# The last V of a decode attention: from four loads and single-column matmuls to one load and four-column matmuls, with the FFN between its parts

## The chip, the cores and the metric

The kernel runs on one core of a Trainium2 chip. The metric is device time of one execution in microseconds, as the median of the fast runs. "Span" is the time from the first to the last instruction of one profiled execution; it is about 2 us less than that execution's time (the profiled run of before: span 1285.6, time 1287.6). Ratios are the mean time of one kernel's fast runs over the mean of the other kernel's fast runs of the same rounds, with a 95% interval, so they are not quite the ratio of the medians quoted beside them.

## The reference

One token of decode: layer norm of x (640), attention with 32 heads over a cache of 32768 positions with head size 128, and beside it a SwiGLU FFN with 1728 hidden units on the same normalised x; everything is added.

```python
xn = layernorm(x)
q = (xn @ wq)                     # 32 heads x 128
p = softmax(q @ k.T * 128**-0.5)  # per head, 32768 keys
o = p @ v                         # per head
out = x + concat(o) @ wo + (silu(xn @ w_gate) * (xn @ w_up)) @ w_down
```

All tensors are bf16. K and V are 8 MiB per head each; everything together is 554 MB, read once.

## The kernel before

K and V of the heads pass through a ring of three 8 MiB slots. A head's scores are made by VectorE (multiply) and TensorE (sum over the head dimension by an identity matmul). Probabilities P lie with key `p * 256 + j` at partition p, column j. V is multiplied in two ways. For heads 0 to 30, four columns j are taken at once ("four-column form"): the weights are 128x4, the moving data are 512 columns of V, and the wanted sums are the four diagonal blocks of a 4x512 result. ScalarE evacuates it (`o4`) and `fold` adds the blocks. (This cut and the two after it are shortened; comments are added.)

```python
PARTS = [64, 64, 128]; W = 4
def pv_part(h, part):
    ...  # part 0 waits for P, for the bank O to be evacuated, and for V
    for j in range(first, first + PARTS[part], W):
        mm = t.matmul(O, lhsT=P[:, h % PR, j:j + W], rhs=ring[:, s, j * DH:(j + W) * DH],
                      start=(j == 0), stop=(j + W == NJ))

def fold(h):   # four fp32 matmuls
    for m in range(W):
        mm = t.matmul(fold_ps, lhsT=o4[:, m * DH:(m + 1) * DH], rhs=identf[0:W, m:m + 1], ...)
```

Head 31 is different: its V comes in four loads, and V itself is the weight, with one column of P as moving data ("single-column form"). That gives the output as a column, without evacuation and fold.

```python
TAIL = [128, 64, 32, 32]          # 4, 2, 1, 1 MiB, a semaphore each
def pv_last(pieces):
    for i in pieces:
        t.wait_ge(s_tail[i], 16)
        for _ in range(TAIL[i]):
            mm = t.matmul(OL, lhsT=ring[:, s, j * DH:(j + 1) * DH], rhs=P[:, h % PR, j:j + 1],
                          start=(j == 0), stop=(j == NJ - 1))
            j += 1
```

Behind V of head 31 the load queue takes gate, up and down weights and then Wo in six pieces. TensorE's tail:

```python
total(H - 1)
pv_last([0])
fold(H - 2)
pv_last(range(1, len(TAIL))).then_inc(s_pv, 1)
hidden_part(0)                        # gate: 70 single-column matmuls, weights strided by 13 elements
t.wait_ge(s_ob, 1)
t.matmul(op, lhsT=oblk, rhs=fold32)   # transposes all heads' outputs into rows for Wo
hidden_part(1).then_inc(s_f, 1)       # up
down()                                # after SiLU on ScalarE and VectorE
project().then_inc(s_att, 1)          # 160 matmuls, waits for six Wo pieces
```

## Time and profile before

| What | Value |
|---|---|
| time | 1287.2 us median (1287.11 to 1287.53, 4 runs) |
| loads | DMA row full in 39 of 40 slices, 431 GB/s over the span |
| TensorE in the tail (1252.8 to 1283.3) | waits 0.6, 1.9 and 0.7 us for Wo, 0.20 and 1.34 us for "issue" |

From the page of the kernel before, the busy share of the DMA engines in 40 equal slices (9 is 90% or more), the granted TensorE clock in tenths, and one of the instruction queues (packets, MB, share):

```profile
PEclk9799888999888898888998888998888998888995
DMA  9999999999999999999999999999999999999998
q8 instruction: 9, 0.15, 0.0%
```

The loads never pause, so a shorter kernel needs either fewer bytes or a shorter tail behind the last of them.

The chain of waits of the kernel before, near its end (start, us, what; the last two pieces, 0.6 us, are left out):

```profile
1253.03 28.77 DMA ring<-in_A_wo_dram
1281.80 0.05 issue
1281.85 1.49 PE ps L428 x40
```

The chain ends in a Wo load: Wo sets the time, and 1.5 us of matmuls plus 2.3 us of fixed work follow.

TensorE's instructions of the kernel before in order of time (start, us, engine, line, out<-in, shape, count, idle before and what ended it). L349 is V of head 31, L359 a fold, L403 gate and up, L412 down, L428 the projection:

```profile
1252.83 3.46 PE L349 MATMUL ps<-P,ring 128*128 128x1 bf16 x128
1256.22 1.86 PE L359 MATMUL ps<-identf,o 4*128 4x1 f32 x8
1258.01 1.20 PE L349 MATMUL ps<-P,ring 128*128 128x1 bf16 x39
1259.41 2.53 PE L349 MATMUL ps<-P,ring 128*128 128x1 bf16 x89 [0.20 <-issue]
1261.80 2.47 PE L403 MATMUL ps<-xn,ring 128*128 128x1 bf16 x39
1265.61 1.83 PE L403 MATMUL ps<-xn,ring 128*128 128x1 bf16 x31 [1.34 <-issue]
1267.33 4.13 PE L403 MATMUL ps<-xn,ring 128*128 128x1 bf16 x70
1272.92 1.87 PE L412 MATMUL ps<-hcol,ring 128*128 128x1 bf16 x65 [1.46 <-DVE hcol L615]
1276.80 1.23 PE L428 MATMUL ps<-ot,ring 128*128 128x1 bf16 x40 [0.59 <-DMA ring<-in_A_wo_dram]
1279.89 1.22 PE L428 MATMUL ps<-ot,ring 128*128 128x1 bf16 x40 [1.86 <-DMA ring<-in_A_wo_dram]
1281.85 1.48 PE L428 MATMUL ps<-ot,ring 128*128 128x1 bf16 x40 [0.74 <-DMA ring<-in_A_wo_dram]
```

256 matmuls on V take 7.2 us, about 28 ns each, and the two gaps without a cause ("issue") sit exactly 256 instructions apart (89 + 39 matmuls, a weight load and a matmul each).

### The profile page before, as it was taken

What the parts mean: (1) busy time and instruction counts of PE and PEld (TensorE: products, weight loads), DVE (VectorE), ACT (ScalarE), POOL (GpSimd) and SP (SyncE); (2) the same over time, 40 slices, a digit from 0 to 9 for tenths busy, and PEclk for the clock granted to TensorE, in tenths of its full rate; (3) what the DMA queues carried; (4) which work ended last, traced back from release to release, by engine and by line L of the source; (5) the groups of instructions that cost most, each with busy time, mean ns of one, the idle gap of its engine ahead of it and who ended that gap; (6) DMA issues with size and microseconds to landing.
All of it is one profiled execution on the core that took longest, in us unless ns stands there. A gap on an engine that the chain in (4) does not pass through costs nothing.

```text
span 1285.6 us, 9851 instructions
## 1 busy us (share of the span) xinstructions
PE 1042.0 (81%) x5154; PEld 260.9 (20%) x3235; DVE 672.2 (52%) x409; ACT 52.1 (4%) x139; POOL 2.5 (0%) x17
## 2 busy tenths in 40 slices
PE   3599777889787799778788777898777798778797
PEld 1012112221112221112221112221112221112227
DVE  0855665445665446664446664446664446654441
ACT  2000000000000000000000000000000000000000
POOL 0000000000000000000000000000000000000000
PEclk9799888999888898888998888998888998888995
DMA  9999999999999999999999999999999999999998
GB/s 424 425 445 433 427 430 441 428 432 440 432 432 428 440 430 430 442 430 432 428 440 430 430 442 430 432 428 440 430 430 442 430 432 428 440 430 430 442 413 365
DMA packets 11256, 554.17 MB, mean 431 GB/s; under 512 B 1259, under 2 KB 1516, under 8 KB 1772
## 3 DMA queue, kind: packets, MB, share of 16 engines
q1 hardware_dynamic: 11242, 554.00, 99.7%
q8 instruction: 9, 0.15, 0.0%
q14 instruction: 3, 0.02, 0.0%
q10 hardware_dynamic: 2, 0.00, 0.0%
HBM read 553.99 MB, written 0.00 MB: 431 GB/s over the span
## 4 chain that ended last, share of the span: by engine, by line
DMA 53%; PE 28%; DVE 12%; issue 6%; SPq 0%; DVEq 0%
DMA ring<-in_A_k_cache_dram 51%; PE ps L337 17%; DVE ring L554 12%; PE ps L305 9%; DMA ring<-in_A_wo_dram 2%; PE ps L324 1%; PE ps L379 0%; PE ps L373 0%; PE ps L367 0%; PE ps L428 0%; SPq L249 0%; DVEq L554 0%; DVE sc L560 0%; DVE pmax L566 0%; DVE m L569 0%
## 5 line engine op out<-in xcount | busy, mean ns | idle before, releaser
L554 DVE TENSOR_TENSOR ring<-ring,qb 128x8192 bf16<-128x8192 bf16 x128 | 557.8, 4420 | 315.6 <-DMA ring<-in_A_k_cache_dram 315.6
L305 PE MATMUL ps<-ring,ident 128*128 128x512 bf16 x1920 | 498.4, 418 | 0.0
L337 PE MATMUL ps<-ring,P 128*4 128x512 bf16 x1984 | 443.3, 379 | 0.0
L324 PE MATMUL ps<-ring,ident 128*128 128x512 bf16 x128 | 56.1, 439 | 220.1 <-DVE ring L554 219.7
L337 PEld LDWEIGHTS ps<-ring,P 128*4 128x4 bf16 x1984 | 163.4, 85 | 237.8
L324 PEld LDWEIGHTS ps<-ring,ident 128*128 128x128 bf16 x128 | 12.6, 99 | 618.3 <-DVE ring L554 359.5
L560 DVE TENSOR_REDUCE sc<-ps 128x64 f32<-128x512 f32 x128 | 82.2, 683 | 63.4 <-PE ps L305 63.4
L572 DVE TENSOR_SCALAR negb<-ps 128x1 f32<-128x1 f32 x32 | 5.1, 159 | 108.4 <-PE ps L379 108.4
L480 ACT ACTIVATE P<-sc,negb 128x256 bf16<-128x256 f32 x32 | 16.2, 507 | 957.7 <-DVE negb L572 957.7
L569 DVE TENSOR_REDUCE m<-ps 1x1 f32<-1x128 f32 x32 | 8.9, 279 | 85.2 <-PE ps L373 85.2
L359 PEld LDWEIGHTS ps<-identf,o 4*128 4x128 f32 x248 | 30.7, 190 | 13.1 <-issue 13.1
L359 PE MATMUL ps<-identf,o 4*128 4x1 f32 x248 | 33.3, 251 | 0.0
L367 PEld LDWEIGHTS ps<-rsum,ones 128*128 128x128 f32 x64 | 12.1, 190 | 99.7 <-issue 98.9
L471 ACT ACTIVATE o<-ps,rzb 4x512 f32<-4x512 f32 x31 | 21.0, 678 | 6.2 <-PE ps L337 6.2
L297 PE MATMUL ps<-ring 128*128 128x512 bf16 x39 | 10.4, 428 | 10.8 <-DMA ring<-in_A_wq_dram 10.7
L476 ACT ACTIVATE ocol<-ps 128x1 f32 (+1 forms) x31 | 5.4, 173 | 222.4 <-PE ps L359 222.4
L566 DVE TENSOR_REDUCE pmax<-sc 128x1 f32<-128x256 f32 x32 | 13.4, 420 | 0.0
L373 PE MATMUL ps<-identf,pmax 128*1 128x128 f32 x64 | 12.2, 273 | 1.2 <-DVE pmax L566 1.2
L379 PE MATMUL ps<-m,ones 1*128 1x1 f32 x64 | 12.1, 256 | 0.4 <-DVE m L569 0.4
L379 PEld LDWEIGHTS ps<-m,ones 1*128 1x128 f32 x64 | 9.4, 182 | 14.2 <-issue 13.5
L403 PE MATMUL ps<-xn,ring 128*128 128x1 bf16 x140 | 8.3, 196 | 1.3 <-issue 1.3
L542 DVE RECIPROCAL rzb<-ps 128x1 f32<-128x1 f32 x32 | 5.0, 157 | 8.1 <-PE ps L367 8.1
(66 smaller groups left out, 82.5 us busy)
## 6 DMA issues: line engine op xcount, KB each, us to landing
ring<-in_A_wq_dram SPq DMA_DIRECT2D x1, 5120.0 KB, 15.2
ring<-in_A_v_cache_dram SPq DMA_DIRECT2D x1, 4096.0 KB, 31.8
ring<-in_A_wo_dram SPq DMA_DIRECT2D x3, 1280.0 KB, 24.7
ring<-in_B_w_gate_dram SPq DMA_DIRECT2D x1, 2160.0 KB, 23.2
ring<-in_B_w_up_dram SPq DMA_DIRECT2D x1, 2160.0 KB, 27.9
ring<-in_B_w_down_dram SPq DMA_DIRECT2D x1, 2080.0 KB, 31.3
ring<-in_A_v_cache_dram SPq DMA_DIRECT2D x1, 2048.0 KB, 36.4
ring<-in_A_v_cache_dram SPq DMA_DIRECT2D x2, 1024.0 KB, 39.4
```

The source lines that it names most:

```text
L305: return t.add_instruction(mybir.InstMatmult(start_tensor_calc=False, stop_tensor_calc=stop, tile_size=(128, 128), tile_position=(0, 0), l ...
L324: t.matmul(ob, lhsT=ident[:, :], rhs=src, start=True, stop=False)
L337: mm = t.matmul(O, lhsT=P[:, h % PR, j:j + W], rhs=ring[:, s, j * DH:(j + W) * DH], start=(j == 0), stop=(j + W == NJ))
L359: mm = t.matmul(fold_ps, lhsT=o4[:, m * DH:(m + 1) * DH], rhs=identf[0:W, m:m + 1], start=(m == 0), stop=(m == W - 1))
L367: t.matmul(misc[:, 129:130], lhsT=ones[:, :], rhs=rsum[:, h % SR:h % SR + 1], start=True, stop=True).then_inc(s_z, 1)
L373: t.matmul(misc[0:1, 0:128], lhsT=pmax[:, h % SR:h % SR + 1], rhs=identf[:, :], start=True, stop=True).then_inc(s_t, 1)
L379: t.matmul(misc[:, 128:129], lhsT=ones[0:1, :], rhs=m1[0:1, h % SR:h % SR + 1], start=True, stop=True).then_inc(s_b, 1)
L471: a.activation(out=o4[:, :], in_=O, func=ACTF.Copy, scale=rzb[0:W, h % SR:h % SR + 1]).then_inc(s_o4, 1)
L480: a.activation(out=P[:, h % PR, :], in_=sc[:, :], func=ACTF.Exp, bias=negb[:, h % SR:h % SR + 1], scale=c_scale, accum_out=rsum[:, h % SR: ...
L554: v.tensor_tensor(out=kh, in0=kh, in1=q[:, None, :].to_broadcast([128, HF, DH]), op=ALU.mult).then_inc(s_mul, 1)
L560: v.tensor_reduce(out=sc[:, i * HF:(i + 1) * HF], in_=bank[i].rearrange("p (j e) -> p j e", e=G), axis=AX.X, op=ALU.add).then_inc(s_red, 1)
L566: v.tensor_reduce(out=pmax[:, h % SR:h % SR + 1], in_=sc[:, :], axis=AX.X, op=ALU.max).then_inc(s_max, 1)
```

## The change

The intent: treat the last head like the others, so that the tail has one load instead of four and 192 fewer matmuls with as many weight loads, and use gate and up to fill the time between V's parts.

```diff
-                    elif u == LASTV:
-                        ...                      # four loads
                     elif u[0] == "v":            # now head 31 too: one 8 MiB load
 ...
                 total(H - 1)
-                pv_last([0])
+                pv_part(H - 1, 0)
                 fold(H - 2)
-                pv_last(range(1, len(TAIL))).then_inc(s_pv, 1)
+                pv_part(H - 1, 1)
                 hidden_part(0)
+                pv_part(H - 1, 2)
+                hidden_part(1).then_inc(s_f, 1)
+                fold(H - 1)
+                down()
                 t.wait_ge(s_const, 5 + 2 * RB)
                 t.wait_ge(s_ob, 1)
                 t.matmul(op, lhsT=oblk[:, :, :], rhs=fold32[:, :], start=True, stop=True).then_inc(s_op, 1)
-                hidden_part(1).then_inc(s_f, 1)
-                down()
                 t.wait_ge(s_ot, 1)
                 project().then_inc(s_att, 1)
```

(Cut: ScalarE evacuates and copies the column of head 31 as for the others; VectorE builds `oblk` after `hcol`; `acc` moves to bank 1, because `fold_ps` is still in use.)

More of the change, by code (lines that the diff above doesn't have):

```diff
@@ L46, in bass_parallel_sum__gqa_block_cached__swiglu_ffn__decode_kernel @@
     SR = 3
-    TAIL = [128, 64, 32, 32]
     RB = DH // 32
@@ L52, in bass_parallel_sum__gqa_block_cached__swiglu_ffn__decode_kernel @@
     W = 512 // DH
-    assert sum(TAIL) == NJ and sum(PARTS) == NJ and NHF == 4 and (H - H0) % PER == 0 and PER % SLOTS == 0
+    assert sum(PARTS) == NJ and NHF == 4 and (H - H0) % PER == 0 and PER % SLOTS == 0
     assert PER % PR == 0 and PER % SR == 0
@@ L76, in bass_parallel_sum__gqa_block_cached__swiglu_ffn__decode_kernel @@
     WQ_S, FFN_S, WO_S = slot_of[("wq",)], slot_of[("ffn",)], slot_of[("wo",)]
-    LASTV = ("v", H - 1)
     with ExitStack() as es:
@@ L120, in bass_parallel_sum__gqa_block_cached__swiglu_ffn__decode_kernel @@
         s_ffn = [sem(n) for n in ("gate", "up", "down")]
-        s_tail = [sem(f"tail{i}") for i in range(len(TAIL))]
         s_const = sem("const")
@@ L208, in bass_parallel_sum__gqa_block_cached__swiglu_ffn__decode_kernel @@
             O = ps8[0:W, 4, :]
-            OL = ps8[:, 5, 0:1]
             op = ps8[:, 5, 8:8 + OC]
-            acc = ps8[:, 6, 0:NCD]
+            acc = bank[1][:, 0:NCD]
             fold_ps = ps8[:, 6, 8:9]
@@ L228, in sp @@
                         owner[s] = (s_qk, NHF * (u[1] + 1))
-                    elif u == LASTV:
-                        j = 0
-                        for i, n in enumerate(TAIL):
-                            e.dma_start(ring[:, s, j * DH:(j + n) * DH],
-                                        kv_src(A_v_cache, u[1], j, n)).then_inc(s_tail[i], 16)
-                            j += n
                     elif u[0] == "v":
@@ L340, in pv_part @@
                         mm.then_inc(s_pv, 1)
-                def pv_last(pieces):
-                    h = H - 1
-                    s = slot_of[LASTV]
-                    for i in pieces:
-                        t.wait_ge(s_tail[i], 16)
-                        j = sum(TAIL[:i])
-                        for _ in range(TAIL[i]):
-                            mm = t.matmul(OL, lhsT=ring[:, s, j * DH:(j + 1) * DH], rhs=P[:, h % PR, j:j + 1],
-                                          start=(j == 0), stop=(j == NJ - 1))
-                            j += 1
-                    return mm
                 def fold(h):
@@ L500, in act @@
                 column(H - 2)
+                evac(H - 1)
+                a.wait_ge(s_f, 1)
+                a.activation(out=sg[:, 0, :], in_=ffn[:, 0:FB], func=ACTF.Exp, scale=-1.0).then_inc(s_fa, 1)
+                column(H - 1)
                 a.wait_ge(s_op, 1)
                 a.activation(out=ot[:, :], in_=op, func=ACTF.Copy).then_inc(s_ot, 1)
-                a.wait_ge(s_f, 1)
-                a.activation(out=sg[:, 0, :], in_=ffn[:, 0:FB], func=ACTF.Exp, scale=-1.0).then_inc(s_fa, 1)
             @block.vector
@@ L592, in dve @@
                 twice(0)
-                h = H - 1
-                v.wait_ge(s_pv, H)
-                v.wait_ge(s_rz, H)
-                v.tensor_scalar(out=ocol[:, h:h + 1], in0=OL, scalar1=rzb[:, h % SR:h % SR + 1],
-                                scalar2=None, op0=ALU.mult).then_inc(s_ov, 1)
+                twice(1)
                 v.wait_ge(s_const, 5 + 2 * RB)
-                v.wait_ge(s_ov, H + 1)
-                v.tensor_tensor(out=oblk[:, :, :], in0=ocol[:, :, None].to_broadcast([128, H, RB]),
-                                in1=blk[:, None, :].to_broadcast([128, H, RB]), op=ALU.mult).then_inc(s_ob, 1)
-                twice(1)
                 v.tensor_reduce(out=par[:, :], in_=ident[:, :].rearrange("p (f t) -> p t f", t=2),
@@ L616, in dve @@
                                 scalar2=ffn[:, FB + FM:2 * FB], op0=ALU.mult, op1=ALU.mult).then_inc(s_fd, 1)
+                v.wait_ge(s_ov, H + 1)
+                v.tensor_tensor(out=oblk[:, :, :], in0=ocol[:, :, None].to_broadcast([128, H, RB]),
+                                in1=blk[:, None, :].to_broadcast([128, H, RB]), op=ALU.mult).then_inc(s_ob, 1)
                 v.wait_ge(s_xr, 1)
```

## The prediction

> **What bounds the kernel now.** The load stream. The DMA row of the 40 slices is full to the end, at 431 GB/s over the span; the chain of waits ends in a 28.8 us wait for the last Wo load, and the instructions in order of time show the projection waiting 0.6, 1.9 and 0.7 us for Wo pieces until 1281.8 us; 2.3 us more of fixed work follow its last matmul. The tail's loads (11.9 MB of FFN weights and Wo) come behind V of head 31, which lands at about 1254.5 us (issues at 1213.0 to 1214.3 plus 31.8 to 40.4 us), exactly one K and one V period (38.7 us) after the last K. So splitting that load costs no visible bandwidth, and joining it gains none; Wo still lands at about 1281.8.
>
> **What the change does to TensorE.** It has little slack in the tail.
> - Removed: 256 single-column matmuls at 27 to 28 ns (7.2 us). Half of them ran before V had wholly landed (1252.8 to 1256.3). Added: 64 four-column matmuls at 221 ns warm (16 took 3.54 us, 32 took 7.01): 14.1 us, all after 1254.5. That is 6.9 us more work and about 1.8 us later start.
> - Code fetch: the tail shows two gaps put down to issue, 0.20 and 1.34 us, exactly 256 instructions apart. [...]
> - Clock: [...]granted clock drops at 1216.8, rises at 1223.6, drops at 1254.3, all multiples of 3.41 us apart, and it then stays 0.5 through single-column work. Now that matters: part 0 of the last V may begin cold, and gate (4.1 us of single-column work) may cool it before part 2. [...]
> - The op matmul and its copy move behind down, onto the path: about 0.55 us.
>
> **Sum along TensorE.** V at 1254.5; part 0 3.5; fold 1.1; part 1 3.5; gate 4.1; part 2 7.0; up 4.1; SiLU chain to down 1.5 (read: 1271.46 to 1272.92), the last fold hidden in it; down 2.1; op and copy 0.55; projection 4.7; end 2.3. That gives 1289.0 us warm, 1292 with both cold starts, against a span of 1285.6 before. Wo, landed at 1281.8, is then waited for no more: the limit moves from the loads to TensorE. With the 1.7 us between span and measured time: 1290.7 to 1293.7. Strided gate and up weights took 59 ns each at half clock and may be faster warm, up to 2 us.
>
> **Predicted:** 1292.0 us, range 1289.5 to 1294.5; slower by 0.4%. Chances: faster by over 2% 0.01, within 2% 0.97, slower 0.02.
>
> **Shows it right:** everything up to 1250 us unchanged; V landing near 1254.5 and part 0 starting there; 64 matmuls of 128x512 taking 14 to 17.5 us; no wait of the projection on Wo, whose landing stays near 1282; chain of waits ending in PE lines rather than Wo; issue gaps of gate and up gone.
>
> **Would make it wrong:** V's single load landing much later or earlier than 1254.5; gate and up running at 30 ns when warm (1289 to 1290); the clock staying cold through all of part 2 (then 1295 or more); a fetch stall within the projection, whose 320 instructions run at 29 ns; Wo still ending the chain, so that the time hardly moves (1287 to 1288).

The sum came to 1289.0 us without cold starts and 1292 with both; the term for a cold start, up to 1.7 us each, was the author's estimate. The trace of the kernel before bears out the size roughly, but not as a bound: 128x512 matmuls that began at a granted clock of 0.50 at 1220.4, 1181.7 and 1143.1 us stayed there for 3.2, 4.3 and 5.4 us (windows view), some 430 ns apart instead of 221, so they lost about half of that, 1.6 to 2.7 us (an estimate from these numbers). That the 1.5 us of issue gaps would go was a forecast; the sum has gate at 4.1 us, without a gap.

## The result, and the profile after

1294.16 us median (1293.42 to 1294.9, 4 runs) against 1287.2 (1287.11 to 1287.53, 4 runs): ratio 1.0054, 95% interval 1.0036 to 1.0071.

The chain of waits of the changed kernel, from the last load in it (start, us, what; L327 is the four-column form, L337 a fold, L381 gate and up, L390 and L396 down, L406 the projection; a VectorE step before down and the pieces after the projection are left out):

```profile
1212.89 41.49 DMA ring<-in_A_v_cache_dram
1254.38 0.14 issue
1254.51 5.10 PE ps L327 x16
1259.62 0.98 PE ps L337 x8
1260.60 3.54 PE ps L327 x16
1264.14 4.11 PE ps L381 x70
1268.25 8.48 PE ps L327 x32
1276.73 4.12 PE ps L381 x70
1282.30 1.87 PE ps L390 x65
1284.17 0.35 PE ps L396 x6
1284.85 4.47 PE ps L406 x160
```

No Wo load is left in the chain. From the landing of V on, it is TensorE without a pause except the 1.4 us of SiLU (between 1280.85 and 1282.30, in which TensorE does the last fold) and 0.5 us for the op matmul and its copy.

TensorE in order of time, the two places that answer to the gaps and to the Wo waits before:

```profile
1264.07 4.18 PE L381 MATMUL ps<-xn,ring 128*128 128x1 bf16 x70
1284.85 4.46 PE L406 MATMUL ps<-ot,ring 128*128 128x1 bf16 x160 [0.29 <-ACT ot L486]
```

Gate is in one piece (the 1.34 us gap is gone) and the projection runs through in one piece: all of Wo had landed.

The windows view of the changed kernel (stretch, its us, busy us of the engines, granted clock in the third last column):

```profile
1254.00:1255.00 1.00, 0.49 (x2) 0.22 (x3) 0.00 (x0) 0.00 (x0) 0.00 (x0) 0.58 0.93 397
1257.00:1258.00 1.00, 1.00 (x5) 0.40 (x4) 0.00 (x0) 0.00 (x0) 0.00 (x0) 0.72 1.02 432
1267.00:1268.00 1.00, 1.00 (x20) 1.00 (x20) 0.00 (x0) 0.00 (x0) 0.00 (x0) 0.90 1.11 455
1268.00:1269.00 1.00, 1.00 (x10) 0.39 (x10) 0.00 (x0) 0.00 (x0) 0.00 (x0) 0.50 0.84 348
1271.00:1272.00 1.00, 1.00 (x5) 0.38 (x4) 0.00 (x0) 0.00 (x0) 0.00 (x0) 0.89 0.95 399
```

The clock halves at about 1254.2 and comes back at 1257.6, and again from 1267.8 to 1271.2 (worked out from the mean clock of the microseconds in which it changed): both times just before a stretch of four-column matmuls starts (1254.51 and 1268.18). Instructions of part 0 took 5.1 us instead of 3.5, those of part 2 8.5 instead of 7.0.

### The profile page after: what moved, and what is told of

Its sections match the earlier page's. It is cut to its first block, busy times and chain, and to the rows that moved or that the text cites. A ratio compares the mean times of both kernels' runs of the same rounds, so it can differ in the third digit from the quotient of the medians.

```text
span 1291.6 us, 9482 instructions
## 1 busy us (share of the span) xinstructions
PE 1052.5 (81%) x4970; PEld 260.0 (20%) x3051; DVE 672.0 (52%) x408; ACT 53.0 (4%) x141; POOL 2.5 (0%) x17
## 4 chain that ended last, share of the span: by engine, by line
DMA 54%; PE 29%; DVE 11%; issue 6%; DVEq 0%; ACT 0%
DMA ring<-in_A_k_cache_dram 50%; PE ps L327 18%; DVE ring L536 11%; PE ps L295 9%; DMA ring<-in_A_v_cache_dram 3%; PE ps L314 1%; PE ps L381 1%; PE ps L357 0%; PE ps L406 0%; PE ps L351 0%; PE ps L390 0%; PE ps L345 0%; DVEq L536 0%; PE ps L337 0%; PE ps L396 0%
## 5 line engine op out<-in xcount | busy, mean ns | idle before, releaser
L327 PE MATMUL ps<-ring,P 128*4 128x512 bf16 x2048 | 460.6, 381 | 1.7 <-DMA ring<-in_A_v_cache_dram 1.7
L327 PEld LDWEIGHTS ps<-ring,P 128*4 128x4 bf16 x2048 | 169.2, 85 | 249.5 <-issue 5.9
L337 PEld LDWEIGHTS ps<-identf,o 4*128 4x128 f32 x256 | 31.0, 187 | 13.6 <-issue 13.5
L337 PE MATMUL ps<-identf,o 4*128 4x1 f32 x256 | 33.7, 248 | 0.0
L345 PE MATMUL ps<-rsum,ones 128*128 128x1 f32 x64 | 9.0, 210 | 0.0
```

Source lines behind the costliest of these rows:

```text
L345: t.matmul(misc[:, 129:130], lhsT=ones[:, :], rhs=rsum[:, h % SR:h % SR + 1], start=True, stop=True).then_inc(s_z, 1)
```

## The experiments

Twelve kernels ran; all gave the right result and were in the fast state (the one single look, x8, is of unknown state). The rival theories are: A, TensorE is the limit of the tail because the four-column form costs twice the single-column form; B, the single load costs; C, the halved clock costs a part of it; D, it does not; E, the order costs; F, the issue gaps are fetches of code; G, they are not; H, the length of the code as such costs time. (In x6, B says that the form costs nothing and D that the terms do not add.)

### One thing undone at a time

**x1_pieces: four loads again, the rest as changed.**

```diff
-  e.dma_start(ring[:, s, :], kv_src(A_v_cache, 31, 0, NJ))
+  four loads of 128, 64, 32, 32 columns; pv_part waits for each as it gets there
```

> The changed kernel, but V of head 31 loaded in the four pieces of before (4, 2, 1, 1 MiB); the multiplication stays in four-column form and in the new order. Theory A (TensorE is the limit of the tail, because 64 four-column matmuls cost 14 us or more where 256 single-column ones cost 7): part 0 can start at about 1252.8 instead of 1254.5 us and starts warm, so about 3.2 us come back: 1291.0 us (1290 to 1292), and the projection still waits for no Wo. Rival B (the one 8 MiB load is what costs, the form does not): back to 1287.3 us.

Measured: 1292.17 us (1291.03 to 1293.17), ratio 1.0038 (1.0021 to 1.0055), 0.2 us over the range of theory A and far from B. Part 0 ran warm, as said, but began late:

```profile
1253.71 3.61 PE L338 MATMUL ps<-ring,P 128*4 128x512 bf16 x16 [0.59 <-issue]
```

Of the 3.2 us expected 2.0 came back. Part of what was missing is a cost of the form that I had overlooked: all heads share the result bank, and ScalarE evacuates head 30 from it only by about 1253.6. The single-column form writes elsewhere and began at 1252.83. A bank of its own brought the start to 1252.90 (x6 below).

**x2_one_load: the kernel before, with one load.**

```diff
-  four loads and four semaphores
+  one load; pv_last waits for it
```

> The kernel before, but V of head 31 in one 8 MiB load; single-column form and order stay. Theory A: all of the 7.2 us of V work now starts at about 1254.4, 1.6 us later, but TensorE had 3 us of waits for Wo, so the time is set by the landing of Wo: 1286.6 to 1287.4 us; if the 0.5 us by which the loads after V landed earlier in the changed kernel belong to the single load, it is 1286.7. Rival B (the single load costs): 1290 us or more.

Measured: 1287.8 us (1287.36 to 1287.88), ratio 1.0002 (0.9986 to 1.0019). B falls. It is 0.4 us over the range of A, and the trace shows why: the projection no longer waits for Wo, but stands still for 1.97 us that the profile puts down to issue (by theory F, a wait for code).

```profile
1276.95 2.44 PE L421 MATMUL ps<-ot,ring 128*128 128x1 bf16 x81
1281.36 2.24 PE L421 MATMUL ps<-ot,ring 128*128 128x1 bf16 x79 [1.97 <-issue]
```

**x5_columns: the changed kernel with only the form undone.** One load, the new order, as much code as before.

```diff
-  pv_part(H-1, 0) ... pv_part(H-1, 1) ... pv_part(H-1, 2) ... fold(H-1)
+  pv_cols(0) ... pv_cols(1) ... pv_cols(2)      # single columns into OL, no fold
-  evac(H-1); column(H-1)                        # ScalarE
+  ocol[:, 31] = OL * rzb                        # VectorE, as in the kernel before
```

> The changed kernel with one thing undone: V of head 31 is multiplied in single columns again (one load, gate and up still between its parts, code as long as before). Theory A (the four-column form is what costs): the V work falls from 17.1 to about 7.2 us, the projection ends with Wo or with a fetch of code instead of being late, and the time is 1287.3 to 1289.0 us, best guess 1288.5, because two waits for code of about 1.7 and 2 us appear 256 instructions apart. Rival E (the new order, gate and up between the parts and op behind down, is what costs): 1291 us or more.

Measured: 1287.15 us (1287.05 to 1287.17) against 1287.24 (1287.13 to 1287.63) of the kernel before, ratio 0.9999 (0.9982 to 1.0015). The interval does not touch that of the changed kernel. E falls. TensorE waits for Wo again:

```profile
1281.39 1.47 PE L420 MATMUL ps<-ot,ring 128*128 128x1 bf16 x40 [0.18 <-DMA ring<-in_A_wo_dram]
```

So undoing the form alone gives back the whole 7 us of medians (1294.16 - 1287.15 = 7.0): with the single-column form, load and order together are worth nothing that can be told from zero, because Wo sets the time. The costs do not simply add: with the four-column form in place, TensorE sets the time, and then four loads give back 2.0 us (x1) and another order 1.8 us (x3 below). My guess of 1288.5 assumed two gaps of 1.7 and 2 us (x2 had shown 1.34 and 1.97); they were 0.80 and 0.40.

### The clock

**x3_gate_after: gate behind all of V.**

```diff
                 pv_part(H - 1, 1)
-                hidden_part(0)
                 pv_part(H - 1, 2)
+                hidden_part(0)
                 hidden_part(1)
```

> The changed kernel, with gate moved behind the last part of V instead of between the parts. Theory C (gate's 4.1 us of single-column work cools the clock, and the last part then starts at half clock for 7 matmuls): part 2 takes 7.0 us instead of 8.5, time about 1292.7 us. Rival D (the order does not matter, clock phases average out): 1294.2 us within 0.5.

**x4_busy_wait: seven useless wide matmuls during the wait for V.**

```diff
                 total(H - 1)
+                t.wait_ge(s_red, NHF * H)
+                for _ in range(7):
+                    t.matmul(bank[2], lhsT=ident[:, :], rhs=qb[:, 0:512], start=True, stop=True)
                 pv_part(H - 1, 0)
```

> The changed kernel, with seven 128x512 matmuls of no use (into a free PSUM bank) run on TensorE in the 1.6 us wait for V. Theory C [...]: part 0 takes 3.6 us instead of 5.1, time about 1292.7 us. Rival D (clock phases average out over executions, or the first matmuls are slow for another reason): 1294.2 us or, if the filler delays part 0, more.

(What is tested is whether part 0 runs warm when TensorE has work in the wait before it.)

Measured: x3 1292.37 us (1290.64 to 1292.76), ratio 1.0040 (1.0023 to 1.0056); x4 1292.77 us (1290.63 to 1293.59), ratio 1.0040 (1.0023 to 1.0057). The medians fall by 1.8 and 1.4 us where 1.5 was forecast. All four times of x3 lie below all four of the changed kernel, those of x4 do not, and both intervals overlap that of the changed kernel. Of x3, part 0, then parts 1 and 2 together:

```profile
1254.52 3.61 PE L327 MATMUL ps<-ring,P 128*4 128x512 bf16 x16 [1.65 <-DMA ring<-in_A_v_cache_dram]
1259.04 10.52 PE L327 MATMUL ps<-ring,P 128*4 128x512 bf16 x48
```

Forty-eight matmuls take 10.5 us, 219 ns each, with no cold stretch; in the changed kernel the same 48 took 3.5 and 8.5. Of x4, the filler, part 0 and part 2:

```profile
1252.82 1.67 PE L421 MATMUL ps<-qb,ident 128*128 128x512 bf16 x7
1254.62 3.61 PE L327 MATMUL ps<-ring,P 128*4 128x512 bf16 x16
1266.80 8.62 PE L327 MATMUL ps<-ring,P 128*4 128x512 bf16 x32
```

For part 2, C is shown: with gate in front of it, part 2 ran partly cold in all three traces (8.5 us in the changed kernel, 8.6 in x4, 8.8 in x1), and with no gate in front parts 1 and 2 took 10.52 us, all warm, in all five (x3, x6, x7, x10, x13).

For part 0, C is not shown. With the useless work in front of it part 0 was 1.5 us shorter, but in the profiled run of x3 it ran just as warm (3.61 us) after the same idle wait and without any filler, so that the span of x3, 1288.7, shows both savings. Where the changes of the granted clock fall seems to decide. In each of the four traces read for it (before, changed, x1, x4) they lie multiples of 3.41 us apart: in the changed kernel at 1216.6, 1223.4, 1254.2, 1257.6, 1267.8, 1271.2 and 1281.5, which is 2, 9, 1, 3, 1 and 3 times 3.41 (worked out from the windows view as above). Counted back in such steps from the drops at 1273.2 (x3) and 1266.6 (x4), a possible place of a change is 1252.7 and 1252.9 (estimates), nearly the same, so x4 might have been warm without its filler; in the changed kernel the clock dropped at 1254.2, just before part 0. Two of the four runs of x4 have spans of 1291.4 and 1291.7 us, about the changed kernel's shortest (1291.5), which does not fit a filler that always helps. A test of the filler would have to compare profiles with the changes in the same place; none here does.

A busy TensorE did not keep the clock up here: in the changed kernel the single-column matmuls of gate kept the matmul row full (1.00 us of each us) from 1265 to 1268, and the clock halved at 1267.8.

The place of these changes also fits the wide spread of x1, x3 and x4 and the narrow one of x6 (1288.57 to 1289.14), where V starts at once and no gate lies between; that they cause the spread is an inference, since only one execution of each kernel was profiled.

### All terms at once, and the way out

**x6_four_best: the four-column form with every other cost taken away.**

```diff
+  four loads; head 31 into its own bank (bank 2)
   pv_part(H-1, 0); fold(H-2); pv_part(H-1, 1)
-  hidden_part(0); pv_part(H-1, 2); hidden_part(1); fold(H-1); down(); op
+  pv_part(H-1, 2); hidden_part(0); hidden_part(1); fold(H-1); down() with op in its middle
```

> Four-column form with every other cost found so far taken away: four pieces; a PSUM bank of its own for head 31, so that part 0 does not wait for the evacuation of head 30 (in the four-piece run it began at 1253.7 instead of 1252.8 us); the three parts together, gate behind them; op in the middle of down. Theory A as a sum: start 1252.9, 64 matmuls at 221 ns and a fold 15.2, gate and up 8.3, last fold 1.9, down and op 2.2, projection 4.5, end 2.3 give a span of 1287.3, a time of 1289.2 us (1288.2 to 1290.2), still over the kernel before. If the terms do not add (Rival D), 1291 us or more; if the form is no cost (Rival B), 1287.3 us.

Measured: 1288.73 us (1288.57 to 1289.14), ratio 1.0012 (0.9995 to 1.0029), span 1286.6. The terms add, 0.5 us better than forecast. TensorE still ends the tail (no wait for Wo), 1.5 us of median behind the kernel before; the interval includes 1, but all four times lie above all seven of the kernel before. That is what remains of the form when it is packed as well as I could.

**x7_best_contig and x13_stride4: the same with other weight strides for gate and up.** 13 elements apart in x6, contiguous in x7, 4 apart in x13; the down weights are loaded to match.

```diff
-  lhsT = w[:, c, 0:1664].rearrange("p (m j) -> p m j", j=13)[:, :, j]
+  lhsT = w[:, c, j*128:(j+1)*128]                       # x7; down rows "(j p) n -> p j n"
+  lhsT = w[:, c, 512*(j//4):...]."(m k)"[:, :, j % 4]    # x13, j < 12; down in 5 KB runs
```

> The same, and gate and up read contiguous columns as weights (hidden unit j*128+m instead of m*13+j; the down weights are loaded in 1280-byte runs to match; the result stays right). If the 59 ns of one gate matmul are the stride of its weights, as the same 59 ns at full and at half clock suggest, gate and up take 2.0 us each instead of 4.1 and about 4 us of TensorE time go; the limit is then Wo again: 1286.5 to 1287.5 us unless code fetch (up to 2 us) [...]get in the way. If the stride is not it: as the run before, 1289.2 us.

> The best four-column kernel (1288.73 us, columns of gate and up 13 elements apart) with the hidden units in groups of four, so that the columns of a weight lie 4 elements (8 bytes) apart, and the down weights in 5 KB runs; the result stays right. It is the candidate for beating both kernels with the shorter code: if 8 bytes are loaded like contiguous weights (26 ns a pair in the contiguous run), gate and up take 3.7 us together, Wo's landing is the limit at 1281.4 to 1281.8 us, and the time is 1286.9 to 1287.5 us. If any stride costs the same (59 ns a pair), 8.3 us stay and the time is 1288.7 us or, with the extra down runs, up to 0.5 more.

Gate and up (140 matmuls in one stretch) of x6, x7 and x13:

```profile
1267.88 8.25 PE L396 MATMUL ps<-xn,ring 128*128 128x1 bf16 x140
```

```profile
1267.84 3.68 PE L396 MATMUL ps<-xn,ring 128*128 128x1 bf16 x140
1282.42 1.48 PE L426 MATMUL ps<-ot,ring 128*128 128x1 bf16 x40 [0.72 <-DMA ring<-in_A_wo_dram]
```

```profile
1267.86 4.52 PE L400 MATMUL ps<-xn,ring 128*128 128x1 bf16 x140
1281.68 0.58 PE L430 MATMUL ps<-ot,ring 128*128 128x1 bf16 x16 [0.74 <-DMA ring<-in_A_wo_dram]
1282.56 0.78 PE L430 MATMUL ps<-ot,ring 128*128 128x1 bf16 x24 [0.29 <-issue]
```

The 59 ns are the stride: 26 ns contiguous, 32 ns at 4 elements. In both, TensorE stops being the limit and Wo is waited for again. Times: x7 1288.2 us (1288.09 to 1288.47), ratio 1.0008 (0.9991 to 1.0024); x13 1287.85 us (1287.46 to 1288.49, 5 runs), ratio 1.0004 (0.9991 to 1.0018). Both miss their first guess by 0.4 to 0.7 us at the upper side. In x7 the last Wo wait ends at 1282.4 instead of 1281.4 (x5). The likely reason, not tested alone: the down load in 1280-byte runs takes 1536 packets more (12778 in all against 11242) and Wo is issued 12 us later (1263.5). In x13 a gap of 0.29 us put down to issue remains. Neither beats the kernel before.

### The code

**x8_shifted and x11_shifted_again: the kernel before, with 128 more instructions at the start.** **x12_whole_block: with 256 more. x10_four_long: x6 with 384 more.**

```diff
+                for _ in range(64):      # 128 in x12, 192 in x10; in the wait for wq, which lasts to 15.3 us
+                    t.matmul(bank[6][0:1, 30:31], lhsT=one1[:, :], rhs=one1[:, :], start=True, stop=True)
                 t.wait_ge(s_a, 11)
```

> The kernel before with 64 tiny matmuls (128 instructions) put into TensorE's wait for wq at the start, where they cost nothing. Theory F (the short gaps in the tail are waits for the next block of 256 instructions of code): every gap moves 128 instructions forward, so gaps come no more in the 39th matmul of the second half of V and the 39th of gate, but near the 103rd matmul of the first half of V, the 103rd of its second half, and the 32nd of up[...]. Rival G (the gaps belong to the data, to semaphores or to the matmuls at that place): they stay where they are. Time within 1.5 us of the kernel before either way.

> The kernel of the shifted run, unchanged, now timed: that one look gave 1288.82 us with the second and third Wo piece landing 1.3 us later than in the kernel before, which no theory of mine had said. If it was chance of that execution: 1287.3 us within 0.4. If the place of the block boundaries does it: 1288.8 us again.

> The kernel before with 128 tiny matmuls (256 instructions, one whole block) in the same wait. Theory F: the gaps stay in the 39th matmul of the second half of V and the 39th of gate, as in the kernel before. Time 1287.3 us within 0.4 if only the place of the boundaries matters; if the extra block of code itself slows the loads, 1287.8 us or more.

> The best four-column kernel (1288.73 us) [...]192 tiny matmuls (384 instructions) in the wait for wq at the start, where they cost nothing. If the length of the code as such is worth time (Rival H), it is slower by 0.5 us or more. Theory A: [...]1288.7 us within 0.4.

The gaps of x11 (128 instructions more):

```profile
1258.05 2.90 PE L351 MATMUL ps<-P,ring 128*128 128x1 bf16 x103
1261.60 0.83 PE L351 MATMUL ps<-P,ring 128*128 128x1 bf16 x25 [0.65 <-issue]
1262.29 4.13 PE L405 MATMUL ps<-xn,ring 128*128 128x1 bf16 x70
```

The gaps of x12 (256 more):

```profile
1258.09 1.20 PE L351 MATMUL ps<-P,ring 128*128 128x1 bf16 x39
1260.13 2.54 PE L351 MATMUL ps<-P,ring 128*128 128x1 bf16 x89 [0.84 <-issue]
1262.53 2.47 PE L405 MATMUL ps<-xn,ring 128*128 128x1 bf16 x39
1266.61 1.83 PE L405 MATMUL ps<-xn,ring 128*128 128x1 bf16 x31 [1.62 <-issue]
```

F holds where gaps showed: in x8 and x11 the gap moved to matmul 103 of the second half (the gaps expected in the first half and in up did not show), and with 256 instructions added both gaps came back to the 39th matmuls. G falls. Successive gaps end about 6.2 us apart in the kernel before (1259.41 to 1265.61) and 6.5 in x12 (1260.13 to 1266.61). That TensorE waits for code there is an inference: the profile says only "issue".

The times were a surprise. x8 1288.82 us (one run); x11 1288.59 us (1288.26 to 1288.61), ratio 1.0009 (0.9992 to 1.0025); x12 1288.65 us (1288.33 to 1288.95), ratio 1.0010 (0.9993 to 1.0026); the kernel before in the same rounds as the last two 1287.34 us (1287.18 to 1287.44). Both intervals include 1, but all four times of x11 and of x12 lie above all seven of the kernel before. So 128 or 256 instructions more, in a place where TensorE has nothing to do, cost 1.3 us, wherever the gaps fall. The loss comes at the end: V of head 31 still starts at 1252.86 to 1252.92 in the three, against 1252.83. In all three the last Wo wait ends about 1.1 us later than the kernel before's 1281.85: 1283.04, 1282.93 and 1282.90. One more instruction packet is moved on q8 (10 against 9), too little to take 1.1 us of the whole stream (9 packets are 0.15 MB, so one is some 17 KB, 0.04 us at 431 GB/s, an estimate). The windows view narrows it down: from 1282.4 to 1283.4 the DMA share is 0.06 in x8 and x11 and 0.07 in x12 (22 to 26 GB/s), but 0.00 in the kernel before. That is the share of about one of the 16 engines, so it looks as if the stream is not slower as a whole, but one engine is still loading when the others have finished, and the last Wo pieces end late with it (an inference from the share). Why that engine is late is open: the profile does not say which engine a packet used, and from 1200 us on all four kernels move five packets on q8, so the extra packet comes earlier.

x10 took 1289.57 us (1289.42 to 1289.8), 0.84 us more than x6; theory A had said at most 0.4, H at least 0.5. (The two were timed in different rounds, in which the medians of the kernel before differ by 0.10 us.) The likely cause is visible: a gap of 0.98 us put down to issue in the projection, which in x6 runs through in one piece of 4.41 us:

```profile
1279.95 2.06 PE L428 MATMUL ps<-ot,ring 128*128 128x1 bf16 x72
1282.99 2.49 PE L428 MATMUL ps<-ot,ring 128*128 128x1 bf16 x88 [0.98 <-issue]
```

## Why the prediction was right

The forecast was 1292.0 us with 1289.5 to 1294.5; 1294.16 lies inside, near the upper end. The direction and the mechanism were right, and the centre was 2.2 us low.

| Step of the prediction | Said | Measured in the changed kernel's trace |
|---|---|---|
| V lands, part 0 starts | 1254.5 | 1254.51 |
| part 0, fold, part 1 | 3.5, 1.1, 3.5, perhaps 1.7 more for a cold start | 5.1, 0.98, 3.54 |
| gate, part 2, up | 4.1, 7.0, 4.1, perhaps 1.7 more for a cold start | 4.11, 8.48, 4.12 |
| SiLU, down, op and copy, projection | 1.5, 2.1, 0.55, 4.7 | 1.45, 2.1, 0.47, 4.47 |
| end | 2.3 | 2.3 |
| span | 1289.0 warm, 1292 with both cold starts | 1291.6, both cold |
| projection waits for Wo | no | no; back as soon as the form is undone (x5) |
| issue gaps of gate and up | gone | gone |

- **The limit moves from loads to TensorE.** Right, and x5 shows that the form does it. As long as Wo sets the time, the single load costs nothing visible (x2), nor does the order (x5); once the form has made TensorE the limit, both cost about 2 us of median (x1, x3).
- **Cold starts.** Right in place and nearly in size: 1.5 us each instead of up to 1.7, read from the trace. That gate causes the one before part 2 is shown by x3; what causes the one before part 0 is not shown by x4. In the changed kernel's trace the clock was at half from 1254.2 to 1257.6 and from 1267.8 to 1271.2, 3.4 us each, and the two drops are 13.6 us apart, four times 3.4.
- **The term that was mis-sized is the centre.** The text left "up to 2 us" for gate and up running faster on a warm clock, and put its centre about midway between no cold start and two. Neither held. Gate and up took 59 ns a matmul at granted clock 1.00 (4.11 us) as at 0.50 (4.13 us), because the cost is the weights' stride (x7, x13). The sum with both cold starts was the right one to take. Chance has a part in this: in x3 part 0 was warm after the same wait, and the changed kernel with a warm part 0 would have taken about 1292.7 us (an estimate, 1294.2 less 1.5), near the forecast.
- **The step from span to time** was taken as 1.7 us, it seems by subtracting a profiled span from the time of other runs. The profiled run itself said 2.0, and 2.2 in the changed kernel. That is another 0.5 us.
- **The code.** That the gaps are fetches of code fits (x8, x11, x12): they move with the count of instructions. That fewer instructions are worth only those gaps is not supported: 128 or 256 more cost 1.3 us in the kernel before. In the changed kernel any such gain lay where it could not help, since TensorE ended the tail and Wo was no longer waited for.
- **Missed:** part 0 also has to wait for the evacuation of head 30 from the shared bank. The single load hid it; it showed in x1 (part 0 at 1253.71 instead of 1252.83 us).

## What to carry to other kernels

A form that is best in a loop bound by loads can be the wrong one in its tail: 64 four-column matmuls at 220 ns cost 14 us where 256 single-column ones cost 7, and here the Wo load, which had landed by about 1281.4 (x5), no longer hid it. Before moving narrow matmuls between wide ones, count the restart of the clock: 1.5 us each time here. Whether useless wide work in an idle wait pays for itself was not settled. Look for gaps put down to issue too: between matmuls of 28 to 59 ns TensorE stood still 0.2 to 2.0 us at places about 256 instructions apart, or double that, where one kernel shows two.
